# Batch 1's first quarter of M beside batch 0's, other PSUM banks in batch 0's first product, and batch 2's tokens whole ahead of the last quarter of w_out

## The chip, the cores and the metric

The kernel runs on one core of one Trainium2 chip, as one program. The metric is the device time of one execution in microseconds (us). The core has five engines that run side by side, each with its own stream of instructions in program order: TensorE (PE, matrix products, with weight loads PEld that overlap them), VectorE (DVE), ScalarE (ACT), GpSimd (POOL) and SyncE (SP). POOL and SP are used here mostly to issue DMAs. Products land in PSUM, which has eight banks of 128 x 512 fp32, and are copied to SBUF by DVE or ACT.

## The reference

The inputs are x (8 batches, 8 heads, 512 tokens, 64 wide), state (8, 8, 32, 64) and two weights w_in (512 x 2048) and w_out (2048 x 512), all fp32. For each batch and head:

```
scores  = (x @ state.T) / 8          a  = softmax(scores)     xread = a  @ state      # 512 x 64
scores2 = (state @ x.T) / 8          a2 = softmax(scores2)    sread = a2 @ x          # 32 x 64
rows    = concat([xread, sread])     # heads side by side: 8 * 544 rows of 512
h = rows @ w_in;  g = max(0.01 * h, h);  out = g @ w_out
```

## The kernel before

The kernel never forms xread. For each batch b it forms M = state (block by head) times w_in, so that h = a @ M. Heads come in two groups g of four, so M is a tile of 128 x 2 x 2048 in bf16, and a (transposed, normalised) a tile aT of 128 x 2 x 512.

- **M in quarters.** `a_m(a, c, tag)` (matmuls at L384) makes quarter c, 512 of the 2048 columns, of batch a's M in two PSUM banks with eight matmuls on 64 x 32 tiles of the array; it needs quarter c of w_in. `tag` names the banks: "sc" and "big" are a pair of banks each, one buffer; "ph" and "py" are single banks, two buffers each. `m_evict` (L396 for single banks, L398 for a pair) copies the quarter to SBUF with the engine it is given.
- **First product.** `ff1` (L405; `ff1_0`, L630, for batch 0) multiplies aT by 128 columns of M, in two matmuls of 512 columns (one for each g); an activation (L410; `relu0`, L638 and L642, for batch 0) applies the leaky relu and writes h in bf16. Sixteen such steps j make h (hT, in batch 0 `h0`). Batch 0 does them two at a time, as j = 0, 2, 4, ... 14.
- **Second product.** `piece(b, hT, i, jq)` (L433) does four of the sixteen matmuls of output tile i (128 rows), with rows 4 jq to 4 jq + 3 (in blocks of 128) of w_out; `y_store` (L442, L448) copies and stores the finished tile. In batch 0, tiles 2 and 3 lie in the pair `wide` ("big" banks, rows named pyw), tiles 0 and 1 in "py" banks.
- **Softmaxes.** `a_scores` (L248) makes scores2 in the pair "sc", `a_max2` and `a_exp2` (L308, L314) their softmax; `a_shift`, `a_exp`, `a_probs` (L258 to L290) the softmax that ends in aT. Batch 0 has its own short form (`scores0` to `probs0`).
- **Tokens.** x[0] comes on SP's queue. x[1] comes as two halves (`x1`, L580), is cast by DVE (L667) and transposed on PE (L684). x[2] (`xl`) comes as two halves by `load_x_half` (L104), is cast by ACT and POOL (L126), and is transposed by two DMAs on SP's queue (`a_xt_half`, L232). Later batches come whole.

Every engine's order is the program order, written out by hand (`tc.manual_schedule`); the tile framework adds the waits and gives banks of one tag in turn. POOL's DMA queue gets, in this order: four quarters of w_in, the first quarter of w_out, two halves of x[1], three quarters of w_out, two halves of x[2]. There are eight semaphores for these transfers, used in turn, so the ninth to twelfth are issued only when the first to fourth have landed.

The program starts with loads and batch 0's softmax; then batch 0's first product, with the rest of M and batch 0's scores2 between its steps; then three quarters of batch 0's second product, with batch 1's softmax; then a loop over batch 1's first product with pieces of the second product between its steps, and a loop for batches 2 to 7 of the same form. A short stage for the 256 state rows of all batches ends it.

Of the kernel before, what the change touches and what calls it, by code (L numbers as in the profile page):

```python
# [9 lines left out]
P = 128  # L10
B, H, S, D = 8, 8, 512, 64
NS = 32
DFF = 2048
DM = 512
SROW = S + NS
NT = S // P
NK = H // 2
# [3 lines left out]
FP32 = mybir.dt.float32  # L21
# [6 lines left out]
def kernel(  # L28
# [9 lines left out]
    nc = tc.nc  # L38
# [3 lines left out]
    xpool = ctx.enter_context(tc.tile_pool(name="xpool", bufs=4))  # L42
# [10 lines left out]
    VEC, SCA, POO = nc.vector.tensor_copy, nc.scalar.copy, nc.gpsimd.tensor_copy  # L53
# [40 lines left out]
    w_out_bf = wpool.tile([P, 16, DM], BF16, name="w_out_bf")  # L94
    xs, xt, xl = {}, {}, {}

    def load_x(b, eng):
        xl[b] = xpool.tile([P, H, NT * D], FP32, name="xl", tag="xl", bufs=2)
        eng.dma_start(xl[b][:], x[b].rearrange("h (p t) d -> p h (t d)", t=NT))

    def load_x_half(b, u):
        if u == 0:
            xl[b] = xpool.tile([P, H, NT * D], FP32, name="xl", tag="xl", bufs=2)
        nc.gpsimd.dma_start(  # L104
            xl[b][:, NK * u:NK * (u + 1)],
            x[b, NK * u:NK * (u + 1)].rearrange("h (p t) d -> p h (t d)", t=NT),
        )

    def open_xb(b):
# [8 lines left out]
    def pair_of(a, t, k):  # L120
        h = 2 * (k % 2)
        return a.xb[k // 2][:, t, h:h + 2, :].rearrange("p h d -> p (h d)")

    def cast_x(b, h0, h1, copy):
        u = h0 // NK
        copy(  # L126
            xs[b][u][:, :, h0 - NK * u:h1 - NK * u].rearrange("p t h d -> p h t d"),
            xl[b][:, h0:h1].rearrange("p h (t d) -> p h t d", t=NT),
        )
# [14 lines left out]
    def load_w_in(c):  # L144
# [2 lines left out]
            moe_w_in[:, DM * c:DM * (c + 1)].rearrange("(k p) f -> p k f", p=P),  # L147
        )

    def load_w_out(c):  # L150
        nc.gpsimd.dma_start(
            w_out_bf[:, 4 * c:4 * (c + 1), :],
            moe_w_out[DM * c:DM * (c + 1), :].rearrange("(j p) f -> p j f", p=P),
        )

    def spin(n, tag):
        p = psum.tile([P, S], FP32, name="pspin", tag=tag, bufs=2 if tag in ("ph", "py") else 1)
# [43 lines left out]
    def state_cast(i):  # L201
        nc.gpsimd.tensor_scalar(
            out=stb[i][:], in0=stf[i][:], scalar1=SCALE, scalar2=None, op0=ALU.mult
        )
# [32 lines left out]
    def st_of(a, g, k):  # L237
        rows = slice(D * g, D * (g + 1))
        if a.b == 0:
            return stbd[rows, k, g ^ (k // 2), :]  # L240
        t = st1 if a.b == 1 else st_t[0][:, a.b - 2] if a.b < 4 else st_t[1][:, a.b - 4]
        return t[rows, NS * k:NS * (k + 1)]

    def a_scores(a):
        sc = psum.tile([P, 2, S], FP32, name="sc", tag="sc", bufs=1)
        for k in range(NK):
            for g in range(2):
                nc.tensor.matmul(  # L248
                    sc[NS * k:NS * (k + 1), g, :],
                    lhsT=st_of(a, g, k),  # L250
                    rhs=a.xTh[k // 2][D * g:D * (g + 1), :, k % 2, :],
                    start=True, stop=True,
                )
        a.sc = sc
# [51 lines left out]
    def a_max2(a):  # L306
        a.m2 = att.tile([P, 2], FP32, name="mcol", tag="mcol")
        nc.vector.tensor_reduce(out=a.m2[:], in_=a.sc[:], axis=AX.X, op=ALU.max, negate=True)  # L308

    def a_exp2(a, g):  # L310
        if g == 0:
            a.e2 = att.tile([P, 2, S], BF16, name="e2", tag="e2")
            a.r2 = att.tile([P, 2], FP32, name="r2", tag="r2")
        nc.scalar.activation(  # L314
            out=a.e2[:, g], in_=a.sc[:, g, :], func=AF.Exp,
            bias=a.m2[:, g:g + 1], accum_out=a.r2[:, g:g + 1],
        )
# [54 lines left out]
    def a_m(a, c, tag):  # L372
        if c == 0:
            a.M = mpool.tile([P, 2, DFF], BF16, name="M", tag="M")
        if tag in ("ph", "py", "phpy"):
            pm = [psum.tile([P, DM], FP32, name="pm", tag=t) for t in (tag[:2], tag[-2:])]
            at = [t[:] for t in pm]
        else:
            pm = psum.tile([P, 2, DM], FP32, name="pm", tag=tag, bufs=1)
            at = [pm[:, g, :] for g in range(2)]  # L380
        for k in range(NK):
            for g in range(2):
                v, r = (k // 2, 2 * (k % 2) + (g ^ (k // 2))) if a.b == 0 else (g, k)
                nc.tensor.matmul(  # L384
                    at[v][NS * r:NS * (r + 1)],
                    lhsT=st_of(a, g, k),
                    rhs=w_in_bf[D * g:D * (g + 1), k, DM * c:DM * (c + 1)],
                    start=True, stop=True,
                )
        return pm  # L390

    def m_evict(a, c, pm, copy):
        cols = slice(DM * c, DM * (c + 1))
        if isinstance(pm, list):
            for g in range(2):
                copy(a.M[:, g, cols], pm[g][:])  # L396
        else:
            copy(a.M[:, :, cols], pm[:])  # L398
# [25 lines left out]

    ys = {}

    def piece(b, hT, i, jq, bank=None, copy=SCA):
        if jq == 0:
            y = ys[b, i] = Y()
            y.py = psum.tile([P, DM], FP32, name="py", tag="py")[:] if bank is None else bank  # L430
        y = ys[b, i]
        for j in range(4 * jq, 4 * jq + 4):
            nc.tensor.matmul(  # L433
                y.py, lhsT=hT[:, j, P * i:P * (i + 1)], rhs=w_out_bf[:, j, :],
                start=(j == 0), stop=(j == 15),
            )
        if jq == 3 and copy is not None:
            y_store(b, i, copy)
# [31 lines left out]
    a0, a1, a2 = att_of[:3]  # L470
# [73 lines left out]
    def sum0(u):  # L544
        r0[u] = psum.tile([P, NG], FP32, name="r0", tag="ph")
        for t in range(NT):
            nc.tensor.matmul(
                r0[u][:, NK * t:NK * (t + 1)], lhsT=e10[u][:, P * t:P * (t + 1)], rhs=ones4,
                start=True, stop=True,
            )  # L550
# [28 lines left out]
    for u in range(2):  # L579
        nc.gpsimd.dma_start(  # L580
            x1[u][:], x[1, NK * u:NK * (u + 1)].rearrange("h (p t) d -> p h (t d)", t=NT)
        )
    for c in range(1, 4):
        load_w_out(c)
    for u in range(2):
        load_x_half(2, u)
    a0.aT = att.tile([P, 2, S], BF16, name="aT", tag="aT")
    open_xb(1)
    a_open(a1, 1)
# [14 lines left out]
    sum0(0)  # L604
    q = [recip0(0)]
    pm = a_m(a0, 0, "sc")
    for g in range(2):
        SCA(a0.M[:, g, :DM], pm[:, g, :])
    sum0(1)
    q.append(recip0(1))  # L610
    for u in range(2):
# [7 lines left out]
    h0 = hpool.tile([P, 16, S], BF16, name="hT", tag="hT")  # L619

    def open_ff1_0(tag):
        if tag == "sc":
            pr = psum.tile([P, 2, S], FP32, name="php", tag=tag, bufs=1)
            return pr, [pr[:, 0], pr[:, 1]]
        ph = [psum.tile([P, S], FP32, name="ph", tag=tag) for _ in range(2)]
        return ph, [p[:] for p in ph]
# [8 lines left out]
    def relu0(t, j):  # L635
# [5 lines left out]
        else:  # L641
            nc.scalar.activation(  # L642
                out=h0[:, j:j + 2, :], in_=t[:], func=AF.Prelu, scale=1 / SCALE, alpha=0.01
            )

    t0, b0 = open_ff1_0("py")
    t2, b2 = open_ff1_0("sc")
    ff1_0(b0, 0, 0)
    ff1_0(b2, 2, 0, (0,))
    ff1_0(b0, 0, 1)  # L650
# [1 line left out]
    ff1_0(b2, 2, 1)  # L652
    relu0(t0, 0)
    relu0(t2, 2)
    m_evict(a0, 2, a_m(a0, 2, "big"), VEC)
    m_evict(a1, 0, a_m(a1, 0, "ph"), VEC)
    for j, tag in ((4, "py"), (6, "sc"), (8, "py"), (10, "ph"), (12, "py"), (14, "ph")):
        t, bk = open_ff1_0(tag)
        for g in range(2):
            ff1_0(bk, j, g)  # L660
        relu0(t, j)
        if j == 8:
            m_evict(a0, 3, a_m(a0, 3, "big"), VEC)
            a_scores(a0)
            a_max2(a0)
    for u in range(2):
        VEC(  # L667
# [5 lines left out]

    for g in range(2):
        a_exp2(a0, g)
    for i in (0, 1):
        piece(0, h0, i, 0)
    wide = psum.tile([P, 2, DM], FP32, name="pyw", tag="big", bufs=1)
    for u in range(2):
        ps = psum.tile([P, NT, 2, P], BF16, name="pxt2", tag="ph")  # L680
        for t in range(NT):
            for v in range(2):
                h = NK * u + 2 * v
                nc.tensor.transpose(  # L684
                    ps[:, t, v, :], pair_of(a1, t, h // 2), ident[:]
                )
        VEC(a1.xT[:, :, 2 * u:2 * u + 2, :], ps[:])
        piece(0, h0, 2 + u, 0, bank=wide[:, u])
    a_scores(a1)
    m_evict(a1, 1, a_m(a1, 1, "ph"), SCA)  # L690
    a_shift(a1)
# [8 lines left out]
    open_xb(2)  # L700
    a_open(a2, 2)
    cast_x(2, 0, 4, SCA)
    state_cast(0)
    cast_x(2, 4, 6, SCA)
    cast_x(2, 6, 8, POO)
    for u in range(2):
        a_xt_half(a2, u)
    state_t(0)
    load_x(3, nc.sync)
    open_xb(3)  # L710
    for g in range(2):
        a_exp2(a1, g)
    a_probs(a1)
    for i in range(NT):
        piece(0, h0, i, 2)
    for i in (2, 3):
        piece(0, h0, i, 3, copy=None)
    for i in (2, 3):
        y_store(0, i, VEC)
    cast_all(3)  # L720
# [6 lines left out]
    for s in range(16):  # L727
        ff1(a1, h1, s)
        if s % 2:
            pb, hT, i, jq = fill[s // 2]  # L730
# [16 lines left out]
        elif s == 13:  # L747
            a_probs2(a1)
            a_a2t_pair(0)
            pm = [a_m(a2, 1, "big"), a_m(a2, 2, "sc")]  # L750
# [6 lines left out]
    for b in range(2, B):  # L757
        hT = hpool.tile([P, 16, S], BF16, name="hT", tag="hT")
        a = att_of[b]
# [4 lines left out]
        for s in range(16):  # L764
# [31 lines left out]
            if nxt is not None:  # L796
# [7 lines left out]
                elif s == 10:  # L804
                    pm0 = a_m(nxt, 0, "big")
                    pm2 = a_m(nxt, 2, "phpy")
                    pm1 = a_m(nxt, 1, "sc")
# [6 lines left out]
            pb, i, jq = order[s]  # L814
# [6 lines left out]
    b = B - 1  # L821
# [43 lines left out]
```

## Time and profile before

| | |
|---|---|
| median of 3 runs | 216.14 us (215.84 to 216.18) |
| profiled execution | 216.04 us, of which the span of its instructions is 213.8 us |
| granted TensorE clock | 0.998 of full speed |
| busy: PE, ACT, DVE, POOL | 206.6 us (97%), 137.5 (64%), 97.9 (46%), 24.9 (12%) |
| mean DMA rate over the span | 130 GB/s |

Busy time by stage, from the table of windows (us from the span's start):

| window | what runs | length | PE busy | DVE | ACT |
|---|---|---|---|---|---|
| 0 to 12.60 | loads, batch 0's softmax | 12.60 | 10.14 | 5.44 | 6.00 |
| 12.60 to 22.05 | batch 0's first product | 9.45 | 8.89 | 7.12 | 7.05 |
| 22.05 to 36.58 | batch 0's second product, batch 1's softmax | 14.53 | 14.42 | 11.18 | 9.69 |
| 36.58 to 58 | batch 1's first product, start of batch 2 | 21.42 | 21.32 | 17.27 | 17.88 |

A row of the timeline gives the start of a group of instructions, the time from the group's first start to its last end, engine, line, operation, output<-input, shape and count; in brackets the idle time before it and what ended it. Matmuls are pipelined, so their rows overlap. The chain of waits is the path that ended last, followed back from the last instruction. In the view of one tile, "DMA to landing" is the time from a transfer's issue to its landing.

### The profile page before, as it was taken

What the parts mean: (1) busy time and instruction counts of PE and PEld (TensorE: products, weight loads), DVE (VectorE), ACT (ScalarE), POOL (GpSimd) and SP (SyncE); (2) the same over time, 40 slices, a digit from 0 to 9 for tenths busy, and PEclk for the clock granted to TensorE, in tenths of its full rate; (3) what the DMA queues carried; (4) which work ended last, traced back from release to release, by engine and by line L of the source; (5) the groups of instructions that cost most, each with busy time, mean ns of one, the idle gap of its engine ahead of it and who ended that gap; (6) DMA issues with size and microseconds to landing.
All of it is one profiled execution on the core that took longest, in us unless ns stands there. A gap on an engine that the chain in (4) does not pass through costs nothing.

```text
span 213.8 us, 3681 instructions
## 1 busy us (share of the span) xinstructions
PE 206.6 (97%) x1482; PEld 96.7 (45%) x1508; DVE 97.9 (46%) x144; ACT 137.5 (64%) x261; POOL 24.9 (12%) x38
## 2 busy tenths in 40 slices
PE   7889999999999999999999999999999999999994
PEld 2533534444444444444444444444444454466543
DVE  1668597697848245741784095706581000000001
ACT  3468567997788476856696578647774766454420
POOL 8831002030033030002100030000000000000000
PEclk9999999999999999999999999999999999999999
DMA  5999995785993981199216921422124110111123
GB/s 178 224 207 293 209 278 115 183 276 111 251 200 95 169 260 49 52 186 222 82 52 148 246 103 49 97 50 100 41 70 86 60 72 18 49 52 49 49 52 98
DMA packets 39872, 27.70 MB, mean 130 GB/s; under 512 B 24496, under 2 KB 35120, under 8 KB 39856
## 3 DMA queue, kind: packets, MB, share of 16 engines
q1 hardware_dynamic: 34912, 21.04, 37.5%
q0 software_dynamic: 4800, 6.29, 14.5%
q8 instruction: 12, 0.20, 0.4%
q10 hardware_dynamic: 144, 0.13, 0.2%
q14 instruction: 4, 0.03, 0.1%
HBM read 17.30 MB, written 8.91 MB: 123 GB/s over the span
## 4 chain that ended last, share of the span: by engine, by line
PE 90%; DMA 5%; POOL 2%; issue 1%; DVE 1%; ACT 0%; POOLq 0%; ACTq 0%
PE py L433 50%; PE ph L405 23%; DMA w_in_bf<-in_moe_w_in_dram 5%; PE pm L384 4%; PE ph L416 3%; PE pyw L433 3%; PE ph L630 2%; PE psr L357 2%; PE pyh L457 2%; PE sc L248 1%; POOL w_in_bf L145 1%; DVE M L398 1%; PE pxt L684 0%; PE php L630 0%; POOL zeroed L82 0%
## 5 line engine op out<-in xcount | busy, mean ns | idle before, releaser
L433 PE MATMUL py<-w_out_bf,hT 128*128 128x512 bf16 x444 | 116.4, 380 | 1.0
L410 ACT ACTIVATE hT<-ph 128x512 bf16<-128x512 f32 x112 | 66.5, 602 | 40.2 <-PE ph L405 39.5
L433 PEld LDWEIGHTS <-hT 128*128 128x128 bf16 x496 | 46.7, 98 | 57.0 <-issue 5.3
L405 PE MATMUL ph<-aT,M 128*128 128x512 bf16 x223 | 65.3, 379 | 0.1
L405 PEld LDWEIGHTS <-M 128*128 128x128 bf16 x224 | 21.7, 98 | 27.0 <-issue 1.4
L442 ACT COPY ysb<-py 128x512 f32<-128x512 f32 x31 | 18.1, 585 | 10.7 <-PE py L433 10.7
L258 DVE TRANSPOSE_TENSOR_REDUCE mrow<-sc 128x32 f32<-128x1024 f32 x7 | 8.8, 1250 | 33.3 <-PE sc L248 33.3
L462 DVE COPY ysh<-pyh 128x384 f32<-128x384 f32 x1 | 0.6, 557 | 49.0 <-PE pyh L457 49.0
L132 POOL CAST xb<-xl 128x2048 bf16<-128x2048 f32 x5 | 9.5, 1892 | 75.1 <-DMA xl<-in_x_dram 41.0
L398 ACT CAST M<-pm 128x1024 bf16<-128x1024 f32 x13 | 13.2, 1013 | 1.2 <-PE pm L384 0.7
L280 DVE TRANSPOSE_TENSOR_REDUCE r<-e 128x32 f32<-128x1024 bf16 x7 | 8.7, 1245 | 11.1 <-ACT e L275 11.1
L398 DVE CAST M<-pm 128x1024 bf16<-128x1024 f32 x9 | 11.0, 1218 | 1.9 <-PE pm L384 1.9
L314 ACT ACTIVATE e<-sc,mcol 128x512 bf16<-128x512 f32 x16 | 11.2, 703 | 0.0
L396 DVE CAST M<-pm 128x512 bf16<-128x512 f32 x12 | 7.7, 686 | 5.0 <-PE pm L384 5.0
L308 DVE TENSOR_REDUCE mcol<-sc 128x2 f32<-128x1024 f32 x8 | 9.7, 1214 | 0.0
L420 ACT ACTIVATE hs<-ph 128x256 bf16<-128x256 f32 x16 | 6.0, 384 | 4.6 <-PE ph L416 4.4
L266 DVE STREAM_TRANSPOSE mrowb<-mrow 128x1024 f32<-128x1024 f32 x7 | 8.7, 1245 | 0.2
L289 DVE STREAM_TRANSPOSE qb<-qh 128x1024 bf16<-128x1024 bf16 x7 | 8.7, 1245 | 0.2
L268 DVE TENSOR_TENSOR sh<-sc,mrowb 128x1024 f32<-128x1024 f32 x7 | 8.6, 1225 | 0.2
L416 PE MATMUL ph<-sr_t,w_in_bf 128*128 128x256 bf16 x64 | 8.3, 273 | 0.0
L638 ACT ACTIVATE hT<-ph 128x512 bf16<-128x512 f32 x12 | 6.4, 598 | 2.5 <-PE ph L630 2.2
L275 ACT ACTIVATE e<-sh 128x1024 bf16<-128x1024 f32 x7 | 7.4, 1051 | 0.6 <-DVE sh L268 0.6
(97 smaller groups left out, 154.3 us busy)
## 6 DMA issues: line engine op xcount, KB each, us to landing
out_dram<-ysb SPq DMA_DIRECT2D x31, 256.0 KB, 2.3
xl<-in_x_dram SPq DMA_DIRECT2D x5, 1024.0 KB, 6.4
w_in_bf<-in_moe_w_in_dram POOLq DMA_DIRECT2D x4, 512.0 KB, 9.3
w_out_bf<-in_moe_w_out_dram POOLq DMA_DIRECT2D x4, 512.0 KB, 16.7
xf<-in_x_dram SPq DMA_DIRECT2D x2, 512.0 KB, 5.1
x<-in_x_dram POOLq DMA_DIRECT2D x2, 512.0 KB, 13.7
xl<-in_x_dram POOLq DMA_DIRECT2D x2, 512.0 KB, 17.0
out_dram<-ysb SPq DMA_DIRECT2D x8, 64.0 KB, 1.7
```

Of the source, the lines that this page charges most:

```text
L132: nc.gpsimd.tensor_copy(xt[b][:].rearrange("p t h d -> p h t d"), xl[b][:].rearrange("p h (t d) -> p h t d", t=NT),)
L258: nc.vector.tensor_reduce(out=m1[:], in_=flat.rearrange("p (c j) -> p c j", j=NS), axis=AX.X, op=ALU.max, apply_transpose=True,)
L266: nc.vector.transpose(m1b[:], m1[:, :, None].to_broadcast([P, n, NS]))
L280: nc.vector.tensor_reduce(out=r1[:], in_=e1[:].rearrange("p (c j) -> p c j", j=NS), axis=AX.X, op=ALU.add, apply_transpose=True,)
L308: nc.vector.tensor_reduce(out=a.m2[:], in_=a.sc[:], axis=AX.X, op=ALU.max, negate=True)
L314: nc.scalar.activation(out=a.e2[:, g], in_=a.sc[:, g, :], func=AF.Exp, bias=a.m2[:, g:g + 1], accum_out=a.r2[:, g:g + 1],)
L398: copy(a.M[:, :, cols], pm[:])
L405: nc.tensor.matmul(ph[:], lhsT=a.M[:, g, P * j:P * (j + 1)], rhs=a.aT[:, g, :], start=(g == 0), stop=(g == 1),)
L410: nc.scalar.activation(out=hT[:, j, :], in_=ph[:], func=AF.Prelu, scale=1 / SCALE, alpha=0.01)
L416: nc.tensor.matmul(ph[:, :n], lhsT=w_in_bf[:, k, P * j:P * (j + 1)], rhs=sr_t[:, k, :], start=(k == 0), stop=(k == NK - 1),)
L433: nc.tensor.matmul(y.py, lhsT=hT[:, j, P * i:P * (i + 1)], rhs=w_out_bf[:, j, :], start=(j == 0), stop=(j == 15),)
L442: copy(ysb[:], ys[b, i].py)
```

## The change

1. **Batch 1's first quarter of M** (`a_m(a1, 0)`) moves from batch 0's first product, where it stood behind `a_m(a0, 2)`, to the place right behind `a_m(a0, 0)`, ahead of batch 0's second `sum0`. It takes the two "py" banks in place of "ph", and ACT copies it in place of DVE.
2. **Batch 0's first product** gets other banks (j = 0 in "sc", 2 in "py", 4 in "ph", 6 and 10 in "big", 8 and 12 in "py", 14 in "ph"). The step j = 4 now stands ahead of `a_m(a0, 2)`, which goes to "sc"; `a_m(a0, 3)` goes to "ph", behind `a_scores(a0)`. DVE copies both in halves of their columns, by a new `m_halves`: two copies of 128 x 2 x 256 for quarter 2, four of 128 x 256 for quarter 3.
3. **Order of batch 0's first pieces**: tiles 2 and 3 first, then tiles 0 and 1, each behind one of the transposes of batch 1's tokens.
4. **POOL's queue**: x[2] comes in one transfer, ahead of the last quarter of w_out, which comes in two halves. ACT casts all of x[2] (two halves), and POOL none. The last quarter's pieces of tiles 2 and 3 are split likewise: block rows 12 and 13 for both tiles, then 14 and 15. `a_exp2(a1)` stands ahead of the transposes of x[2] in the text; on each engine this changes no order.

```diff
-    for c in range(1, 4):
-        load_w_out(c)
-    for u in range(2):
-        load_x_half(2, u)
+    load_w_out(1)
+    load_w_out(2)
+    load_x(2, nc.gpsimd)
+    for v in range(2):
+        load_w_out_rows(12 + 2 * v, 14 + 2 * v)
...
     pm = a_m(a0, 0, "sc")
+    pm1 = a_m(a1, 0, "py")
     for g in range(2):
         SCA(a0.M[:, g, :DM], pm[:, g, :])
+    m_evict(a1, 0, pm1, SCA)
     sum0(1)
...
+    def m_halves(a, c, tag):
+        pm = a_m(a, c, tag)
+        for i in range(2):
+            part = slice(2 * P * i, 2 * P * (i + 1))
+            cols = slice(DM * c + 2 * P * i, DM * c + 2 * P * (i + 1))
+            if isinstance(pm, list):
+                for g in range(2):
+                    VEC(a.M[:, g, cols], pm[g][:, part])
+            else:
+                VEC(a.M[:, :, cols], pm[:, :, part])
+
-    t0, b0 = open_ff1_0("py")
-    t2, b2 = open_ff1_0("sc")
+    t0, b0 = open_ff1_0("sc")
+    t2, b2 = open_ff1_0("py")
...
-    m_evict(a0, 2, a_m(a0, 2, "big"), VEC)
-    m_evict(a1, 0, a_m(a1, 0, "ph"), VEC)
-    for j, tag in ((4, "py"), (6, "sc"), (8, "py"), (10, "ph"), (12, "py"), (14, "ph")):
+    for j, tag in ((4, "ph"), (6, "big"), (8, "py"), (10, "big"), (12, "py"), (14, "ph")):
         t, bk = open_ff1_0(tag)
         for g in range(2):
             ff1_0(bk, j, g)
         relu0(t, j)
-        if j == 8:
-            m_evict(a0, 3, a_m(a0, 3, "big"), VEC)
+        if j == 4:
+            m_halves(a0, 2, "sc")
+        elif j == 8:
             a_scores(a0)
+            m_halves(a0, 3, "ph")
             a_max2(a0)
...
-    for i in (0, 1):
-        piece(0, h0, i, 0)
     wide = psum.tile([P, 2, DM], FP32, name="pyw", tag="big", bufs=1)
+    for u in range(2):
+        piece(0, h0, 2 + u, 0, bank=wide[:, u])
     for u in range(2):
...
         VEC(a1.xT[:, :, 2 * u:2 * u + 2, :], ps[:])
-        piece(0, h0, 2 + u, 0, bank=wide[:, u])
+        piece(0, h0, u, 0)
...
     cast_x(2, 0, 4, SCA)
+    cast_x(2, 4, 8, SCA)
     state_cast(0)
-    cast_x(2, 4, 6, SCA)
-    cast_x(2, 6, 8, POO)
...
-    for i in (2, 3):
-        piece(0, h0, i, 3, copy=None)
+    for v in range(2):
+        for i in (2, 3):
+            piece(0, h0, i, 3, copy=None, js=range(2 * v, 2 * v + 2))
```

`load_w_out_rows(j0, j1)` issues one transfer of block rows j0 to j1 - 1 of w_out; `load_w_out(c)` calls it for a quarter. `piece` takes `js`, the matmuls of the four to do.

More of the change, by code (lines that the diff above doesn't have):

```diff
@@ L99, in load_x @@
         eng.dma_start(xl[b][:], x[b].rearrange("h (p t) d -> p h (t d)", t=NT))
[L101 to L107, printed above, removed]
     def open_xb(b):
@@ L148, in load_w_in, with load_w_out_rows @@
         )
+    def load_w_out_rows(j0, j1):
+        nc.gpsimd.dma_start(
+            w_out_bf[:, j0:j1, :], moe_w_out[P * j0:P * j1, :].rearrange("(j p) f -> p j f", p=P)
+        )
     def load_w_out(c):
[L151 to L154, printed above, removed]
+        load_w_out_rows(4 * c, 4 * (c + 1))
     def spin(n, tag):
@@ L425, with piece @@
     ys = {}
-    def piece(b, hT, i, jq, bank=None, copy=SCA):
+    def piece(b, hT, i, jq, bank=None, copy=SCA, js=range(4)):
         if jq == 0:
@@ L431, in piece @@
         y = ys[b, i]
-        for j in range(4 * jq, 4 * jq + 4):
+        for j in [4 * jq + v for v in js]:
             nc.tensor.matmul(
@@ L621, in open_ff1_0 @@
     def open_ff1_0(tag):
-        if tag == "sc":
+        if tag in ("sc", "big"):
             pr = psum.tile([P, 2, S], FP32, name="php", tag=tag, bufs=1)
@@ L702 @@
     cast_x(2, 0, 4, SCA)
+    cast_x(2, 4, 8, SCA)
     state_cast(0)
-    cast_x(2, 4, 6, SCA)
-    cast_x(2, 6, 8, POO)
+    for g in range(2):
+        a_exp2(a1, g)
     for u in range(2):
@@ L710 @@
     open_xb(3)
-    for g in range(2):
-        a_exp2(a1, g)
     a_probs(a1)
```

## The prediction

> **What bounds the kernel now.** I read the page's busy shares first, then the share of the chain of waits by engine, then the chain in order of time over the first 37 us, then PE's timeline there.
>
> ```profile
> PE 206.6 (97%) x1482; PEld 96.7 (45%) x1508; DVE 97.9 (46%) x144; ACT 137.5 (64%) x261; POOL 24.9 (12%) x38
> PE 90%; DMA 5%; POOL 2%; issue 1%; DVE 1%; ACT 0%; POOLq 0%; ACTq 0%
> ```
>
> PE is 97% busy and carries 90% of the chain. So the time is PE's work plus its few waits, and a microsecond saved on PE early lasts to the end, if what PE needs next comes early enough too. The rest of the chain lies at the start:
>
> ```profile
> 4.50 10.71 DMA w_in_bf<-in_moe_w_in_dram
> ...
> 15.26 0.63 PE pm L384 x16
> ...
> 18.62 0.39 PE pm L384 x8
> 19.03 1.24 DVE M L398
> 20.27 0.05 issue
> 20.31 1.90 PE ph L630 x8
> ```
>
> PE waits twice in batch 0's first product: at 15.26 for the third quarter of w_in (landed at 15.2), and at 20.31 for DVE's copy of M's last quarter. PE's timeline prices the steps:
>
> ```profile
> 13.67 0.60 PE L630 MATMUL ph<-aT,M 128*128 128x512 bf16 x2
> 14.10 0.81 PE L630 MATMUL php<-aT,M 128*128 128x512 bf16 x3
> 15.26 0.41 PE L384 MATMUL pm<-w_in_bf,stbd 64*32 64x512 bf16 x8 [0.35 <-DMA w_in_bf<-in_moe_w_in_dram]
> 15.49 0.40 PE L384 MATMUL pm<-w_in_bf,st 64*32 64x512 bf16 x8
> 15.82 1.04 PE L630 MATMUL ph<-aT,M 128*128 128x512 bf16 x4
> 16.69 1.03 PE L630 MATMUL php<-aT,M 128*128 128x512 bf16 x4
> ...
> 28.88 0.41 PE L384 MATMUL pm<-w_in_bf,st 64*32 64x512 bf16 x8
> 29.22 1.90 PE L433 MATMUL pyw<-w_out_bf,hT 128*128 128x512 bf16 x8
> 31.05 0.41 PE L384 MATMUL pm<-w_in_bf,st 64*32 64x512 bf16 x8
> ```
>
> A full matmul takes 0.216 us of PE's flow (16.69 less 15.82, over four). Eight matmuls and one lone M quarter take 31.05 - 28.88 = 2.17, so the lone quarter takes 2.17 - 1.73 = 0.44. A second tiled group behind the first costs only 15.49 - 15.26 = 0.23 more.
>
> **Part 1, batch 1's quarter moved.** In the first product it leaves one lone quarter where a pair stood: 0.21 to 0.23 saved; I take 0.21. At its new place PE stands idle: batch 0's first quarter starts at 10.94, and the next matmuls (L547) start at 11.53, behind DVE's reciprocal. The pair would be through at about 10.94 + 0.23 + 0.32 = 11.49, so I take nothing; the bounds are 0 (no gain, as the path there runs over ACT and DVE) and 0.2, what it costs if that wait were gone. ACT, which now copies it, has finished batch 0's quarter at 12.5 and then waits 1.59 us until 14.09 for its first relu; two copies (the row of two at L608 has 1.07) end at 13.5, ahead of it. DVE loses two copies, 1.28 us.
>
> **Part 2, j = 4 ahead of the third quarter.** The eight matmuls of j = 0 and 2 end at 14.75. PE then enters the quarter at 15.26, less some 0.09 for the change of tile shape: 0.42 us of wait. j = 4 needs M's second quarter, which DVE copies from 13.47 to 14.69, so its four matmuls run from 14.75 to 15.61. The third quarter starts at 15.70, after w_in's landing, and "sc" is free by then (relu of j = 0, about 14.3 to 15.33). The wait of 0.42 goes. Next late could be:
>
> - j = 8 at 16.92, for the first half copy. DVE starts 0.46 after the last matmul of a quarter (15.28 to 15.74 before), so at 16.19; one copy of 512 elements has 0.64 (the pair of L396 below), so 16.83, just in time.
> - Batch 0's scores2 waited 0.06 for ACT's relu of j = 2 to free "sc"; now "sc" waits for DVE's second half at about 17.5, before 17.88. 0.06 saved.
> - j = 10 at 18.45 for "big": ACT's relus run densely from 14.3, and that of j = 6 ends at 18.2.
>
> **Part 2, last quarter in four copies.** It starts at about 18.08 (w_in's last quarter has landed at 17.7), so DVE starts at 18.57.
>
> ```profile
> 16.89 1.28 DVE L396 CAST M<-pm 128x512 bf16<-128x512 f32 x2
> 19.03 1.23 DVE L398 CAST M<-pm 128x1024 bf16<-128x1024 f32 x1 [0.87 <-PE pm L384]
> ```
>
> No row has a copy of 256 elements. The slope between these rows gives about 0.37 for one, so 0.75 for the first two and 1.5 for four; the upper bound is 0.64 each, 2.6 for four, the lower 0.31 each (half of 0.64), 1.2 for four. I take the slope, as the work is the same copy. j = 12 starts at 19.31, needs the first two for its second half only at 19.7, and has them at 19.3; j = 14, at 20.18, needs all four, and has them at 20.07. The wait of 0.27 for L398 (PE's gap before 20.31, less its pace) goes. At the upper bound j = 14 waits until 21.2: 1.0 us. The Trainium skill's page "Perfetto Trace Analysis", section "Optimizing Scalar/DVE Operations", speaks against small pieces: each DVE instruction on PSUM carries about 125 ns whatever its size. By it, as an estimate, four copies take 0.38 more than the one of 1.23, 1.6 in all, and the sum would lose under 0.05; the two rows agree with it (their slope leaves 0.1 that does not scale).
>
> **Sum of the first product.** 0.42 + 0.27 + 0.06 + 0.21 = 0.96 us. The second product starts at 21.09 in place of 22.05. The other order of tiles costs nothing in itself: as many matmuls, with "big" and "py" free by 20.6 and 21.0.
>
> **Part 3 and 4, can the second product keep the lead?** DMAs do not move with PE. Issue plus time to landing give, before: w_out's quarters at 20.2, 25.6, 28.2 and 31.5, x[1]'s halves at 21.8 and 23.2, x[2]'s at 33.0 and 34.4.
>
> ```profile
> L151 POOL DMA_DIRECT2D w_out_bf<-in_moe_w_out_dram x4: 740/763/796, 7.6 to 12.0; - x4
> DMA to landing us min/median/max: 12.6/16.7/19.5
> ```
>
> The new needs: w_out's first quarter at 21.09; the transposes of x[1]'s halves at 22.8 and 24.1, after casts that end at 22.5 and 23.9; second quarter at 26.1; third at 30.4. All hold, the closest by 0.2. DVE's softmax of batch 1 starts and ends with its scores, about 1 us earlier, so aT is there at 34.9 and needed at 35.6.
>
> POOL's queue carries the same bytes in as many transfers. x[2] takes the place of w_out's last quarter, so it lands near 31.5, not 34.4; ACT casts it from 31.8 to 33.7 (1.04 for each half, from L126). SP's transposes are then issued 1.3 us earlier than before:
>
> ```profile
> 34.14 2.71 SPq L232 DMA_TRANSPOSE xT<-xb  x2
> 36.90 1.24 SPq L207 DMA_TRANSPOSE st_t<-stb  x1
> ```
>
> The last of them (2.4 us to landing) then lands near 38, where batch 2's scores, at 40.13 before, now need it at 39.2. Without the earlier x[2] the landing of 39.3 would eat 0.1.
>
> The price is w_out's last quarter: its halves land near 33.0 and 34.4, and are needed at 33.9 and 34.8. I take no wait; 0.4 us of cover, the thinnest of all. After 36 us nothing else changes: PE is busy 21.32 of 21.42 and 141.06 of 142.00 us in the next windows, and its waits move along with it.
>
> 216.04 of the profiled execution less 0.96 is 215.08; the median of the runs stands 0.10 above that execution, so 215.2. A measurement of this kernel can tell about 0.2% (0.43 us) from no change.
>
> **The rivals.**
>
> Late weights, lead partly eaten. If block rows 14 and 15 land at 35.2 instead of 34.4, PE waits 0.4: 215.6. For it: transfers end ragged here, the third quarter of w_in landing 0.5 us after PE was ready and w_out's last one 3.3 us after its forerunner (2.6 for the others), beside the state's loads on SP's queue; the transposes now come 1.3 us earlier. Against it: the transposes issued at 34.14 land from 37.3 on, so they move little in their first microsecond.
>
> Late weights, slower. The same place: SP's transposes, issued from 32.8 on, hold the DMA engines before w_out's last half is through, and it lands only with them. They took 3.3 us to landing, so 36.1 or later; the kernel is slower from a landing of 35.8 on. At 36.6 it costs 1.8 against the 0.96 gained: 217.0. Against it: the last w_out quarter, beside the state's loads, was stretched by 0.7 and not stopped. By the Trainium skill's "DMA: Bandwidth & Descriptors", section "Queues, rings and completion order", each DMA engine takes turns between its queues packet by packet; by that rule the half is only slowed, and this rival becomes the one before.
>
> DVE's pieces. Four copies at the upper bound make j = 14 wait 1.0: 216.1, no change. For it: a copy of half the size already costs 0.64, not 0.61; against it: the slope.
>
> The quarter doesn't fit. If PE's start stage has no room for it, 0.2 goes back: 215.4; still faster.
>
> **How the numbers follow.** Forecast 0.60 (including the quarter that doesn't fit); lead partly eaten 0.16, of which 0.02 ends within 0.2%; DVE's pieces 0.10; late weights slower 0.08; a clash of banks or queues that the rows don't show 0.06, half of it slower, half no change. So faster 0.74, same 0.15, slower 0.11. The range reaches from 214.8 (the runs' own 0.3 below the forecast, and the pair's upper price) to 216.2 (all of the gain lost); beyond it lie the slower cases.
>
> **What would show it.** PE's third quarter at 15.7 with no DMA wait before it; no DVE wait before j = 14; the first pyw at 21.1; batch 0's piece of rows 14 and 15 without a gap at 34.8; the first ph of L399 (L405 before) at 35.6; batch 2's scores at 39.2. Wrong would be a DMA wait of w_out_bf near 34 to 36, or gaps before j = 8 or j = 14.

## The result, and the profile after

Timed beside the kernel before, the changed kernel has a median of 215.14 us (215.06 to 215.62, 6 runs) against 216.16 us (215.84 to 216.28, 6 runs). The ratio is 0.9959, with a 95% interval of 0.9946 to 0.9971. Two further measurements give 0.9971 [0.9960, 0.9982] (215.57 against 216.15 us) and 0.9957 [0.9943, 0.9970] (215.37 against 216.20 us). So the gain is 1.02, 0.58 and 0.83 us, 0.3 to 0.5%, and no interval reaches 1. The forecast was 215.2 us. The profiled execution took 215.09 us, with a span of 213.0 us. Its page, the same two lines as before:

```profile
PE 208.2 (98%) x1508; PEld 96.8 (45%) x1508; DVE 96.4 (45%) x146; ACT 138.5 (65%) x262; POOL 24.0 (11%) x37
PE 91%; ACT 3%; DVE 2%; DMA 1%; SPq 1%; issue 0%; ACTq 0%
```

PE now carries 91% of the chain, and the transfer of w_in has left it: it had 5%, all DMA together now have 1%. PE's timeline in batch 0's first product (ph and php are the steps j, in single banks and in a pair; the first row has the last three matmuls of j = 2 and the four of j = 4):

```profile
14.20 1.67 PE L627 MATMUL ph<-aT,M 128*128 128x512 bf16 x7
15.80 0.41 PE L378 MATMUL pm<-w_in_bf,stbd 64*32 64x512 bf16 x8
16.14 1.04 PE L627 MATMUL php<-aT,M 128*128 128x512 bf16 x4
17.03 1.04 PE L627 MATMUL ph<-aT,M 128*128 128x512 bf16 x4
18.00 0.41 PE L242 MATMUL sc<-xT,stbd 64*32 64x512 bf16 x8
18.22 0.40 PE L378 MATMUL pm<-w_in_bf,stbd 64*32 64x512 bf16 x8
18.55 1.04 PE L627 MATMUL php<-aT,M 128*128 128x512 bf16 x4
19.43 1.89 PE L627 MATMUL ph<-aT,M 128*128 128x512 bf16 x8
21.15 1.89 PE L427 MATMUL pyw<-w_out_bf,hT 128*128 128x512 bf16 x8
```

There is no bracket in it: j = 4 fills the time before the third quarter, one lone quarter stands at 15.80, and the second product starts at 21.15 (forecast 21.1). DVE's copies of M's third and last quarter, in DVE's timeline (brackets: idle time before, and what ended it):

```profile
16.28 1.29 DVE L652 CAST M<-pm 128x512 bf16<-128x512 f32 x2 [1.55 <-PE pm L378]
18.66 1.42 DVE L650 CAST M<-pm 128x256 bf16<-128x256 f32 x4 [1.10 <-PE pm L378]
```

The second product is as dense as before and ends at 35.69. Then something new shows. SP's timeline, with the start and the length of each issue:

```profile
32.88 3.45 SPq L226 DMA_TRANSPOSE xT<-xb  x2
36.42 1.21 SPq L201 DMA_TRANSPOSE st_t<-stb  x1
```

The chain of waits at that place, which goes through the state's transfer:

```profile
36.42 2.92 DMA st_t<-stb
```

And PE's timeline at the start of batch 2's scores:

```profile
38.28 1.03 PE L427 MATMUL py<-w_out_bf,hT 128*128 128x512 bf16 x4
39.39 0.41 PE L242 MATMUL sc<-xT,st_t 64*32 64x512 bf16 x8
```

The first transpose is issued 1.26 us earlier than before, but the two of the tokens take 3.45 us of SP's queue in place of 2.71. So the state's follows only at 36.42, lands at 39.35, and batch 2's scores, which PE could have begun at 39.23, begin at 39.39. The transposes are now on the chain.

### The profile page after: what moved, and what is told of

The parts are those of the page before. It is cut to its first block, busy times and chain, and to the rows that moved or that the text cites. A ratio compares the mean times of both kernels' runs of the same rounds, so it can differ in the third digit from the quotient of the medians.

```text
span 213.0 us, 3710 instructions
## 1 busy us (share of the span) xinstructions
PE 208.2 (98%) x1508; PEld 96.8 (45%) x1508; DVE 96.4 (45%) x146; ACT 138.5 (65%) x262; POOL 24.0 (11%) x37
## 3 DMA queue, kind: packets, MB, share of 16 engines
q1 hardware_dynamic: 34912, 21.04, 39.2%
## 4 chain that ended last, share of the span: by engine, by line
PE 91%; ACT 3%; DVE 2%; DMA 1%; SPq 1%; issue 0%; ACTq 0%
PE py L427 48%; PE ph L399 22%; PE pm L378 4%; PE ph L410 3%; PE pspin L153 2%; PE ph L627 2%; PE psr L351 2%; PE pyh L451 2%; PE php L627 1%; DMA st_t<-stb 1%; PE sc L242 1%; ACT xb L118 1%; PE pyw L427 1%; ACT e L308 1%; PE pxth L479 1%; DVE mrow L252 1%
## 5 line engine op out<-in xcount | busy, mean ns | idle before, releaser
L427 PE MATMUL py<-w_out_bf,hT 128*128 128x512 bf16 x464 | 118.9, 379 | 0.0
L404 ACT ACTIVATE hT<-ph 128x512 bf16<-128x512 f32 x112 | 66.5, 602 | 40.5 <-PE ph L399 40.5
L390 DVE CAST M<-pm 128x512 bf16<-128x512 f32 x10 | 6.4, 686 | 5.3 <-PE pm L378 5.3
L392 DVE CAST M<-pm 128x1024 bf16<-128x1024 f32 x7 | 8.5, 1215 | 0.0
L378 PE MATMUL pm<-w_in_bf,st_t 64*32 64x512 bf16 x192 | 7.6, 379 | 0.0
```

What stands on the lines that cost most here:

```text
L378: nc.tensor.matmul(at[v][NS * r:NS * (r + 1)], lhsT=st_of(a, g, k), rhs=w_in_bf[D * g:D * (g + 1), k, DM * c:DM * (c + 1)], start=True, st ...
L404: nc.scalar.activation(out=hT[:, j, :], in_=ph[:], func=AF.Prelu, scale=1 / SCALE, alpha=0.01)
L427: nc.tensor.matmul(y.py, lhsT=hT[:, j, P * i:P * (i + 1)], rhs=w_out_bf[:, j, :], start=(j == 0), stop=(j == 15),)
```

## The experiments

Times are medians; each ratio, with its 95% interval, is to the kernel before, timed beside it. "Wait" is what PE waited at batch 2's scores beyond its usual 0.31 us from the last full matmul to a tiled group. The table is read from the profiles; "outside" is the profiled time less the span. A row is one execution. No run has part 2's order of steps or part 3 alone; for these the timelines speak.

| kernel | second product starts | last transpose landed | scores of batch 2 | wait | span | outside |
|---|---|---|---|---|---|---|
| before | 22.05 | 39.28 | 40.13 | 0 | 213.75 | 2.29 |
| before, again | 22.09 | 40.81 | 40.85 | 0.68 | 214.50 | 2.28 |
| changed | 21.15 | 39.35 | 39.39 | 0.16 | 213.04 | 2.05 |
| changed, again | 21.20 | 39.61 | 39.65 | 0.26 | 213.29 | 2.04 |
| changed, third | 21.04 | 39.86 | 39.90 | 0.78 | 213.54 | 2.04 |
| old queue order | 21.03 | 40.15 | 40.20 | 0.73 | 213.82 | 2.27 |
| queue order alone | 22.02 | 39.49 | 40.10 | 0 | 213.73 | 2.03 |
| whole copies | 21.77 | 38.99 | 39.85 | 0 | 213.48 | 2.05 |
| quarter alone | 22.22 | 39.55 | 40.30 | 0 | 213.95 | 2.27 |

In every row the span is the start of batch 2's scores plus 173.62 to 173.65 us. So in these kernels all that the change does to the span is settled there: the scores start when PE gets to them, or 0.04 us after the last transpose has landed, whichever is later.

**The changed kernel and the kernel before, again.**

> The changed kernel again, as the reference for the three beside it. Theory (the gain was made in batch 0's first product, 0.9 us on PE by 35.7 us, of which 0.15 us is lost again where batch 2's scores wait for SP's transpose of the state): ratio to the kernel before 0.9955 to 0.9965, first piece of the second product at 21.1 to 21.2 us, scores of batch 2 at 39.3 to 39.5 us behind a DMA wait of 0.1 to 0.2 us. Rival (the gain is an accident of when w_in's third quarter lands, which was 14.3 us here and 15.2 us in the profile before): where that quarter lands at 15.2 us, the first product is longer by 0.4 us and more.

> The changed kernel once more, as the reference for the three beside it. Theory (0.9 us gained in the first product in every execution, and a part that varies lost again where batch 2's scores wait for SP's transposes): 215.1 to 215.6, ratio to the kernel before 0.995 to 0.998; scores of batch 2 wait by 0.1 to 0.4 us. Rival (a second wait takes the rest): another wait of over 0.1 us after 40 us.

> The kernel before again, for one more look at its profile. Theory: PE waits for VectorE's copy of M's last quarter by about 0.27 us before j = 12 in every execution; its wait for w_in's third quarter is 0.42 us where that lands at 15.2 us and near nothing where it lands before 14.7 us. Rival (the landing is the same in each execution of one kernel): 15.2 us again.

Measured: ratios 0.9971 and 0.9957, as above; the kernel before took 216.78 us in its one execution. PE's timeline at the waits. The kernel before, again:

```profile
15.30 0.41 PE L384 MATMUL pm<-w_in_bf,stbd 64*32 64x512 bf16 x8 [0.27 <-DMA w_in_bf<-in_moe_w_in_dram]
40.85 0.41 PE L248 MATMUL sc<-xT,st_t 64*32 64x512 bf16 x8 [0.61 <-DMA st_t<-stb]
```

The changed kernel, again:

```profile
39.65 0.41 PE L242 MATMUL sc<-xT,st_t 64*32 64x512 bf16 x8 [0.19 <-DMA st_t<-stb]
```

The changed kernel, third:

```profile
39.90 0.41 PE L242 MATMUL sc<-xT,st_t 64*32 64x512 bf16 x8 [0.71 <-DMA st_t<-stb]
```

w_in's third quarter landed at 15.2 us in both profiles of the kernel before, and there PE waited. It landed at 14.3, 15.25 and 14.7 us in the three of the changed kernel, and there PE did not wait in any, as the need has moved to 15.7 and later. The rival, an accident of one landing, falls. The kernel before also waited again by 0.27 us for DVE's copy of M's last quarter. The wait at the scores is in all three of the changed kernel, and was larger than I had taken it (up to 0.78); and the kernel before has it too, in one of its two profiles. In the first repeat the ratio, 0.9971, missed what I had expected (0.9955 to 0.9965): besides the wait at the scores, PE lost 0.11 us at the transposes of batch 1's tokens, whose second half landed at 23.56 in place of 22.37.

**POOL's old order in the changed kernel.**

```diff
...
-    load_x(2, nc.gpsimd)
-    for v in range(2):
-        load_w_out_rows(12 + 2 * v, 14 + 2 * v)
+    load_w_out(3)
+    for u in range(2):
+        load_x_half(2, u)
...
-    cast_x(2, 4, 8, SCA)
     state_cast(0)
+    cast_x(2, 4, 6, SCA)
+    cast_x(2, 6, 8, POO)
```

> The changed kernel with POOL's old order: w_out's last quarter whole, then batch 2's tokens in two halves, the last two heads cast by POOL. Theory (the new order gives almost nothing, since SP's three transposes end near 39.3 us in either order): batch 2's scores wait for the transposes by 0.1 to 0.3 us, and the time is that of the changed kernel within 0.2 us, about 215.2. Rival (the new order is what keeps the lead): the scores wait by 0.5 us or more, 215.6 or above.

Measured: 216.08 against 216.15 us, ratio 0.9993 [0.9983, 1.0003]. My theory falls and the rival holds: without the new order the whole gain is gone. SP's timeline of this kernel, then PE's with its waits in brackets:

```profile
34.55 2.70 SPq L234 DMA_TRANSPOSE xT<-xb  x2
```

```profile
24.41 0.62 PE L700 MATMUL pxt<-ident,xb 128*128 128x128 bf16 x8 [0.19 <-DVE stf L687]
40.20 0.41 PE L250 MATMUL sc<-xT,st_t 64*32 64x512 bf16 x8 [0.66 <-DMA st_t<-stb]
```

PE has the same lead at 21.03 us. It loses 0.35 of it at 24.41 (x[1]'s second half landed late, at 23.64) and the rest at the scores, behind transposes issued 1.67 us later than in the changed kernel. The first of these losses is not the order's doing: x[1] stands in the queue ahead of all that was moved, and PE lost 0.33 us there with the new order too, in one of the kernels further down (scores and exponential later), where x[1]'s second half landed at 23.61:

```profile
24.38 0.62 PE L692 MATMUL pxt<-ident,xb 128*128 128x128 bf16 x8 [0.16 <-DVE stf L679]
```

Against the changed kernel beside it (215.57) the old order costs 0.51 us; 0.23 of that is the time outside the span.

**The new order alone, on the kernel before** (part 4 of the change, nothing else).

```diff
-    for c in range(1, 4):
-        load_w_out(c)
-    for u in range(2):
-        load_x_half(2, u)
+    load_w_out(1)
+    load_w_out(2)
+    load_x(2, nc.gpsimd)
+    for v in range(2):
+        load_w_out_rows(12 + 2 * v, 14 + 2 * v)
...
     cast_x(2, 0, 4, SCA)
+    cast_x(2, 4, 8, SCA)
     state_cast(0)
-    cast_x(2, 4, 6, SCA)
-    cast_x(2, 6, 8, POO)
...
-    for i in (2, 3):
-        piece(0, h0, i, 3, copy=None)
+    for v in range(2):
+        for i in (2, 3):
+            piece(0, h0, i, 3, copy=None, js=range(2 * v, 2 * v + 2))
```

> The kernel before with part 4 alone: batch 2's tokens whole and ahead of w_out's last quarter, which comes in two halves, its pieces split. Theory (nothing before waits for the tokens, and the weights land over 1 us ahead of their need): no change, 216.1 within 0.2. Rival (the weights are late): PE waits before the pieces of rows 12 to 15, 0.3 us or more slower.

Measured: 215.84 against 216.26 us, ratio 0.9981 [0.9972, 0.9990]: 0.4 us faster, where I had expected nothing. The weights are not late. The gain has two parts. The time outside the span is 0.24 us less; see the last section. And the spread is smaller (215.73 to 216.23, against 215.92 to 216.83); that this is because late transposes no longer reach the need at 40.1 is argued from single profiles (landed at 39.49 here, at 39.28 and 40.81 in the kernel before). The parts of the change do not add: parts 1 to 3 without this one gave 0.07 us, this one alone 0.42, together 0.58 to 1.02.

**Whole copies in place of halves.**

```diff
-            m_halves(a0, 2, "sc")
+            m_evict(a0, 2, a_m(a0, 2, "sc"), VEC)
...
-            m_halves(a0, 3, "ph")
+            m_evict(a0, 3, a_m(a0, 3, "ph"), VEC)
```

> The changed kernel with whole copies by DVE: quarter 2 of M in one copy of 1024 elements, quarter 3 in two of 512. Theory (the halves are what lets PE run on): j = 8 waits for the whole copy, 16.28 + 1.23 + 0.05 = 17.55 instead of 17.03, 0.5 us; j = 12 waits another 0.1 us for its second copy; the time is 0.6 us above the changed kernel, about 215.7. Rival (ScalarE's relus pace the first product anyway, so the halves are hidden): within 0.15 us of the changed kernel.

Measured: 215.78 against 216.15 us, ratio 0.9986 [0.9977, 0.9994]. PE's timeline at j = 8:

```profile
17.49 1.04 PE L627 MATMUL ph<-aT,M 128*128 128x512 bf16 x4 [0.39 <-DVE M L392]
```

The gap before j = 8 is 0.76 us, 0.54 more than the pace of 0.22 us a matmul; inside j = 12, ahead of its second half, PE loses another 0.15. The second product starts 0.57 to 0.73 us later than in the three profiles of the changed kernel, as forecast. But the time is only 0.21 above that of the changed kernel beside it (215.57), between theory and rival, and the intervals of the two ratios overlap. In the profile the transposes had landed before PE came: what is lost ahead of a wait is partly hidden by it.

**Batch 1's quarter alone, on the kernel before.**

```diff
     pm = a_m(a0, 0, "sc")
+    pm1 = a_m(a1, 0, "py")
...
+    m_evict(a1, 0, pm1, SCA)
...
-    t0, b0 = open_ff1_0("py")
-    t2, b2 = open_ff1_0("sc")
+    t0, b0 = open_ff1_0("sc")
+    t2, b2 = open_ff1_0("py")
...
-    m_evict(a1, 0, a_m(a1, 0, "ph"), VEC)
-    for j, tag in ((4, "py"), (6, "sc"), (8, "py"), (10, "ph"), (12, "py"), (14, "ph")):
+    for j, tag in ((4, "ph"), (6, "sc"), (8, "py"), (10, "ph"), (12, "py"), (14, "ph")):
```

> The kernel before with batch 1's first quarter of M alone moved (beside batch 0's, in the py banks, copied by ScalarE; j = 0, 2 and 4 in the banks sc, py and ph so that it has room). Theory (a second tiled group behind another costs PE 0.21 us, and in the start stage PE has room for it): 0.2 us faster than before, about 215.95. Rival (it delays the second row sums and so batch 0's softmax): same or slower than before, 216.1 to 216.3.

Measured: 216.10 against 216.26 us, ratio 0.9994 [0.9979, 1.0009], which does not tell 0.2 us from nothing. The trace tells more: from the third quarter's start to the second product it has 22.22 - 15.68 = 6.54 us, the two profiles of the kernel before have 6.79. The 0.25 us is there. The profiled execution as a whole was no faster (span 213.95), as its start stage was 0.8 us late; but that was so ahead of the moved quarter (batch 0's first quarter at 11.72 in place of 10.94), and the matmuls behind the pair follow 0.59 us after the first quarter's start, as before. So the rival, late row sums, is not borne out.

**Weights later.** This makes w_out's last halves late by the order of the queue, to test the price that the prediction put on late weights; batch 3's tokens leave SP's queue for it.

```diff
     load_x(2, nc.gpsimd)
+    load_x(3, nc.gpsimd)
     for v in range(2):
         load_w_out_rows(12 + 2 * v, 14 + 2 * v)
...
     state_t(0)
-    load_x(3, nc.sync)
     open_xb(3)
```

> The changed kernel with batch 3's tokens, too, on POOL's queue ahead of w_out's last quarter, whose landing is then delayed by one transfer of 1 MB. This tests the price that the prediction gave to late weights. Theory: the tokens take 2.7 to 3 us of the queue, so the second half lands at 36.3 to 36.6 us in place of 33.6, PE needs it at 34.9 us and waits 1.4 to 1.7 us; the time is 216.5 to 216.9. Rival (the lead has other cover, or the queue is not in order): under 0.5 us slower than the changed kernel.

Measured: 217.67 against 216.26 us, ratio 1.0061 [1.0047, 1.0076]. PE's timeline shows a wait before each half:

```profile
36.15 0.81 PE L427 MATMUL pyw<-w_out_bf,hT 128*128 128x512 bf16 x3 [1.54 <-DMA w_out_bf<-in_moe_w_out_dram]
37.42 1.02 PE L427 MATMUL pyw<-w_out_bf,hT 128*128 128x512 bf16 x4 [0.46 <-DMA w_out_bf<-in_moe_w_out_dram]
```

The halves landed at 36.11 and 37.38. In the result's profile the last four matmuls of these pieces started at 34.82, and batch 2's scores could have started at 39.23; here they started at 37.42 and 41.83, both 2.6 us later. So the price is the landing less the need. (The brackets add up to less, as the start stage came 0.5 us late in this execution.) My range of 216.5 to 216.9 was too low: I had the tokens' transfer too short (3.2 us, not 2.7 to 3), and the delay of 0.5 us that was in the queue already left out.

**Four tries at the wait for the transposes, on the changed kernel.** Scores of batch 2 one step later; that and the exponential behind them a step later; the state's loads and transpose ahead of the tokens' ones; and the last two together. The first run has the first hunk below, the second run all of the first fence, the third the second fence, the fourth both.

```diff
-        if s == 3:
+        if s == 4:
             a_scores(a2)
...
         elif s == 7:
-            a_exp(a2)
             a_open(att_of[3], 3)
             a_xt_dma(att_of[3])
+        elif s == 8:
+            a_exp(a2)
```

```diff
+    nc.vector.memset(stf[0][:, 0, D - 1:D + 1], 0.0)
+    load_state(0)
     for u in range(2):
         VEC(
...
-    nc.vector.memset(stf[0][:, 0, D - 1:D + 1], 0.0)
-    load_state(0)
...
+    state_t(0)
     for u in range(2):
         a_xt_half(a2, u)
-    state_t(0)
```

> The changed kernel with batch 2's scores, its first quarter of M and the VectorE work behind them one step later in batch 1's first product (behind s = 4 in place of s = 3). Theory (PE waits only for SP's last transpose): the wait of 0.15 us goes, since the scores now stand 0.43 us later, and the time falls by 0.1 to 0.15 us, to about 215.0. Rival (the softmax of batch 2 then becomes late, and ScalarE waits for VectorE's shifted scores with batch 1's relus queued behind it): 0.1 to 0.3 us slower than the changed kernel.

> The changed kernel with batch 2's scores behind s = 4 in place of s = 3, and the exponential that waits for their shifted form behind s = 8 in place of s = 7. Theory (behind s = 4 alone PE lost at s = 9 what it had won, 0.56 us, since ScalarE waited 0.72 us for VectorE with two relus queued behind the exponential): no wait at s = 9 now, the wait for the transposes under 0.1 us, and 0.15 to 0.3 us faster than the changed kernel, 215.1 or below. Rival (batch 2's softmax, now 0.9 us later, becomes late for its first product at 51 us): as slow as the changed kernel or slower.

> The changed kernel with batch 2's and 3's state loaded some 2 us earlier (ahead of VectorE's casts of batch 1's tokens) and transposed ahead of the tokens, not behind them. Theory (three transposes in a row on SP's queue set the landing; one of them can be through before the tokens are cast): the last lands near 38.3 to 38.8 us in place of 39.4 to 39.6, batch 2's scores don't wait, 0.15 to 0.3 us faster than the changed kernel. Rival (the state's loads, earlier, take the DMA engines from w_out's second quarter, due at 26.1 us): PE waits 0.1 to 0.5 us there, and the gain is gone.

> Both of the last two changes. Theory: if the transposes alone make the wait, this is no faster than the better of the two, as either takes it away; PE runs from 12.6 us on without a wait over 0.1 us, about 215.1. Rival (the wait varies so much that neither cover alone is enough): 0.1 us or more faster than either, and with less spread over the runs.

Measured, in this order: ratios 0.9973 [0.9963, 0.9982], 0.9966 [0.9952, 0.9979], 0.9967 [0.9950, 0.9984], 0.9963 [0.9949, 0.9977]; the changed kernel beside the first had 0.9971, beside the others 0.9957. None is faster than the changed kernel. Later scores turn the wait into another; PE's timeline with the scores later:

```profile
45.65 1.08 PE L399 MATMUL ph<-aT,M 128*128 128x512 bf16 x4 [0.40 <-ACT hT L404]
```

And with the exponential later too:

```profile
46.19 0.59 PE L399 MATMUL ph<-aT,M 128*128 128x512 bf16 x2 [0.39 <-ACT hT L404]
```

In both, the gap is 0.55 us longer than the pace, as the exponential (1.06 us) now holds up a relu that frees one of PE's two "ph" banks. My theory for the second of them, that this wait would go, was wrong; the fourth kernel has it too. Loading the state first moves its transpose to 32.3 us, but one of the tokens' then takes 2.3 us to issue, and the last of them lands at 39.70: PE waits 0.42 us in the middle of the scores instead of ahead of them, which makes this row 0.83 long in place of 0.41:

```profile
39.31 0.83 PE L242 MATMUL sc<-xT,st_t 64*32 64x512 bf16 x8
```

## Why the prediction was right, and where not

- **The first product**: forecast 0.96 us, and measured close to it. The third quarter stands at 15.80 with no DMA wait; j = 8 at 17.03 follows the first half copy (16.28 + 0.65) with no wait; four copies took 1.42 us (forecast 1.5, bounds 1.2 and 2.6). The prediction's two rows, taken as shown, leave 0.05 us that does not scale (2 x 0.64 - 1.23), not 0.1, and so give 1.4; its other estimate, 0.38 more for four copies than for one, came out as 0.19 (1.42 against 1.23). PE's lead is 22.05 - 21.15 = 0.90, and 1.01 counted from the start of the stage, which came 0.1 later in this execution (13.12 against 13.01).
- **The quarter's new place costs nothing**: the matmuls behind it follow 0.59 us after the first quarter's start, before (10.94 to 11.53) and now (10.98 to 11.57). ACT's copies end at 13.5, as forecast.
- **The second product keeps the lead**: 21.15 to 35.69 is 14.54 us, as before. w_out's last halves landed at 32.45 and 33.63 (forecast 33.0 and 34.4), more than 1 us ahead of need; in the changed kernel's two other profiles the second half landed at 34.52 and 34.23, which leaves nearly 0.5. The thinner cover was elsewhere: of the needs with "All hold, the closest by 0.2", the one for x[1]'s second half failed in some executions (0.11 us lost in the changed kernel, again). Of the rivals, late weights were wrong here, and "weights later" shows that their price was right; copies at the upper bound fall.
- **The step that failed** is the last one of parts 3 and 4: "The last of them (2.4 us to landing) then lands near 38". It landed at 39.35 to 39.86 and cost 0.16 to 0.78 us. I had moved the transposes as a block by 1.3 us with the issue times of the trace before. In the result's profile the last is 1.33 us later than by that working: it was issued 0.78 later than the block, and took 0.54 longer to land (2.92 in place of 2.38). The same step said that without the earlier x[2] 0.1 us would be lost; "old queue order" lost 0.73 there, and with 0.35 at x[1] and 0.23 outside the span the whole gain was gone. So part 4, which I took for mere cover, decides most of what parts 1 to 3 are worth.
- **What the sum did not have**: 0.24 us less outside the span. In the profiled pair the span fell by 0.71 and the time by 0.95. That the forecast of 0.96 came out is thus partly luck: the wait that I missed and the time outside the span that I missed have opposite signs. The two further measurements gained 0.58 and 0.83.

## What to carry to other kernels

A lead won early on the bounding engine lasts only as far as the next thing that does not move with it; list every landing after it, with its spread over several profiles and not one, and ask for each what its issue will collide with when it comes earlier. Where one event fixes the rest (here the span is the start of batch 2's scores plus 173.6 us in every row of the table), read all experiments at that event: it shows which of two candidates arrived last, and why undoing one part can cost the whole gain.

## What the runs showed of the hardware that was not expected

- **SP's issue of a transpose can stall.** In the four profiles with POOL's old order each tokens' transpose takes 1.23 to 1.34 us to issue. In all with the new order one of the two takes 1.6 to 2.6. The DMA records of each profile have one packet of 16 KB on an instruction queue (q8), 0.9 to 1.6 us long, starting between 32.8 and 34.5 us in all but "weights later". With the old order it is through when the first transpose is issued, or within 0.1 us of that; with the new one it overlaps the slow issue, which ends 0.5 us (the first of the two) or 1.0 to 1.1 us (the second) after the packet, in nine profiles. In "weights later" one took 2.53 us with no such packet at that time, and w_out was still in flight. That the packet blocks the transposes is argued from these times; no run isolates it.
- **The time outside the span** was 2.27 to 2.29 us in the four profiles with POOL's old order, 2.15 in "weights later" and 2.03 to 2.05 in the nine others. It is so in all runs, not only the profiled ones: the means by kernel are 2.30 to 2.36, 2.17, and 2.03 to 2.07. What in the queue's order makes it is open.
- **A tiled group costs PE** 0.44 us alone and 0.23 more behind another one, before and after alike: in the changed kernel eight full matmuls and a lone group take 2.17 us too (27.98 to 30.15), 1.73 of it for the matmuls, and the second group of a pair starts 0.22 to 0.23 behind the first (18.00 to 18.22, 10.98 to 11.21).
